# One step of VectorE's exponentials on GpSimd, other buffer counts and another table of the planner's rules

## The chip, the cores and the metric

The kernel runs on one core of a Trainium2 chip. The metric is the device time of one execution in microseconds, as the median of several runs. Names of engines: PE is TensorE, ACT is ScalarE, DVE is VectorE, POOL is GpSimd, SP is SyncE.

## The reference

The input x has 2048 rows of 512 in bf16. The output mixes an attention block and an MLP by a gate for each row:

```python
x = A_x
g = sigmoid((x * gate_w).sum(-1, keepdims=True))
a = attention(x, wqkv, wo)          # 32 heads of 16, softmax over 2048 keys
b = mixer_mlp(x, w1, w2, w3, w4)    # layernorm, gelu(x@w1), shift rows by quarter of channels, @w2,
                                    # residual, layernorm, gelu(@w3) with 1792 columns, @w4, residual
return g * a + (1 - g) * b
```

The attention has 32 x 2048 x 2048 scores, each of which needs an exponential.

## The kernel before

**Units and slots.** The queries are cut into four chunks of 512 and the heads into eight groups of four, which makes 32 units. A unit has 64 blocks of scores: 16 tiles of 128 keys for each of four heads. TensorE computes the scores of two or three blocks into a PSUM tile (`stage`, line 709; function `score`), ScalarE makes the exponentials of that tile in one instruction (`pt`, line 947; 1024 or 1536 elements per partition), and TensorE multiplies them with the values into an accumulator (`acc`, line 960; `attend_block`). One such round is a slot. Two sets of PSUM banks alternate, so the scores of slot k wait for the exponentials of slot k - 2.

**Quad chains.** Some tiles of keys do not go to ScalarE. Their four heads' scores go one by one into a fourth PSUM tile (`dsc`) in slots that then hold only two blocks for ScalarE. VectorE makes their exponentials by working on the bits of bf16 numbers. Function `whole` posts a chain: four dumps (line 873, `dsc` to int16, 512 wide; the bank is free after it), then on all four heads together, 2048 wide, mantissa (883), square (888), power (893) and a last addition of a constant (898, function `later`). Three of these results, the square, the power and the last sum, are each multiplied with the values into the same accumulator. The buffers of a chain (`quad`, and later also parts of `more` and `xT`) come from a list `room`.

**The other work.** TensorE also makes the projections, the MLP's matmuls (line 223) and the output's; VectorE evacuates PSUM, computes the layernorms' statistics (311, 314) and normalized rows (331) as side jobs (`asides`), and rescales each unit's accumulator (1031 to 1051). ScalarE also makes the GELUs (925, 928) in five groups, with table loads around each. GpSimd only sets constants at the start, raises eight small tiles to a power (321) and makes one addition at the end (1156).

**The order.** A planner in the kernel's own Python runs when the program is built. It keeps a clock for each engine (`free`), a cost for each piece of work and a list of what may come next, picks the earliest by time and rank, and emits the instruction. So the order on each engine's queue is fixed by the planner's costs and rules. `USUAL` and `RULES` hold the rules, by unit: how much work of VectorE's may stand in its queue before a new chain starts (`DLIM`), how many chains may run at once (`CHAINS`), from when on tiles of the next unit may be taken (`NEED`), and when a chain's steps and TensorE's products move up (`AHEAD`, `HURRY`, `MANY`, `PTS`). `CREDIT` and `LATER` set how much of the MLP TensorE may do in each slot. Where TensorE would be idle it gets filling matmuls (`fill`, lines 1259 and 1262). `port` keeps two kinds of work apart in time: work posted as shared on VectorE (the 2048-wide steps, the normalized rows, the rescaling) and all work on GpSimd.

Of the kernel before, what the change touches and what calls it, by code (L numbers as in the profile page):

```python
# [12 lines left out]
ALU = mybir.AluOpType  # L13
# [5 lines left out]
I16 = mybir.dt.int16  # L19
# [8 lines left out]
QUARTER = 32.0 - 3.0 * 128.0  # L28
# [4 lines left out]
def kernel(  # L33
# [14 lines left out]
    P = 128  # L48
# [3 lines left out]
    H = 32  # L52
    DH = D // H
    KT = D // P
    VK = 5
    OB = 8
    PTB = 6
    APART = 8
    STAY = 0

    QS = 128.0 * DH ** -0.5 / LN2
    NT = S // P
# [94 lines left out]

    USUAL = {"NEED": 34, "AHEAD": 16, "HURRY": 14, "DLIM": 1.8, "MANY": 5, "PTS": 4, "CHAINS": 3}  # L160
    RULES = {1: {"NEED": 26, "HURRY": 0, "MANY": 5, "PTS": 6, "CHAINS": 3}, 2: {"NEED": 26, "HURRY": 0, "DLIM": 1.5, "MANY": 4, "PTS": 5}, 4: {"AHEAD": 16, "HURRY": 8}, 6: {"AHEAD": 6, "HURRY": 0, "DLIM": 2.1, "MANY": 4, "CHAINS": 4}, 7: {"MANY": 3, "PTS": 6}, 8: {"NEED": 26, "HURRY": 18, "CHAINS": 3}, 9: {"NEED": 36, "HURRY": 8, "DLIM": 2.1, "MANY": 3, "CHAINS": 5}, 10: {"DLIM": 1.2, "MANY": 5, "CHAINS": 4}, 12: {"NEED": 26, "HURRY": 18, "MANY": 2}, 13: {"HURRY": 8, "PTS": 5}, 14: {"NEED": 28, "AHEAD": 16, "HURRY": 24, "CHAINS": 5}, 15: {"AHEAD": 10, "MANY": 2, "PTS": 5}, 16: {"NEED": 28, "AHEAD": 16, "DLIM": 1.8, "MANY": 2}, 18: {"NEED": 30, "AHEAD": 6, "HURRY": 0, "MANY": 5}, 19: {"NEED": 32, "DLIM": 1.5}, 20: {"AHEAD": 8, "DLIM": 2.1, "MANY": 4, "PTS": 3, "CHAINS": 4}, 21: {"NEED": 32, "AHEAD": 16, "HURRY": 8, "PTS": 5}, 22: {"AHEAD": 8, "HURRY": 18, "MANY": 3, "PTS": 5}, 23: {"NEED": 30, "AHEAD": 12, "HURRY": 14, "DLIM": 2.1, "CHAINS": 4}, 24: {"NEED": 34, "AHEAD": 8, "MANY": 4, "PTS": 5}, 27: {"AHEAD": 10, "DLIM": 1.8, "CHAINS": 4}, 28: {"NEED": 26, "DLIM": 1.5, "MANY": 4}, 29: {"AHEAD": 10, "DLIM": 1.5, "MANY": 5, "CHAINS": 3}, 30: {"NEED": 28, "AHEAD": 10, "DLIM": 1.5, "MANY": 4}, 31: {"NEED": 32, "HURRY": 18, "MANY": 5, "PTS": 6, "CHAINS": 5}}
    MM = 0.2235
    TURN = 0.09
    PE_OUT = 0.43
    WARM = 8
    EARLY = 34
    DUNIT = 1
    MAXD = 16
    LASTNEED = 32
    SPLIT = 12  # L170
    RANGES = ((0, 2), (2, 3), (3, 4))
    SPACE = 1
    CREDIT = 0.45
    LATER = 0.4
    GELU, WTWO = 1.0, 1.6
    MOST = 12.0
    LOAD = 1.3
# [3 lines left out]
    SLACK = 0.3  # L181
    AGE = 2.0
    ARANK = 3
    TANH = 1.5
    NOWFREE = 12.0
    free = {"pe": NOWFREE, "act": NOWFREE, "vector": NOWFREE, "pool": NOWFREE}
    queue = {"pe": [], "act": [], "vector": [], "pool": []}
    state = {"n": 0, "gen": 0, "young": True, "mm": 0, "kind": "", "t": 0.0, "piece": 0.0,
             "credit": 0.0, "mixable": 0, "done": False, "ending": False, "acc": 0.0, "accsb": 0.0, "slot": 0, "outs": 0, "bank": 0}
    asides = deque()  # L190
    at = {}
# [365 lines left out]
    def job_option():  # L557

        if current["job"]:
            return 0.0, current["job"]  # L560
        bank = bank_time()
        if bank is None:
            return None
        options = []
        if urgent and urgent[0].hold() is not None:
            options.append((max(urgent[0].hold(), bank), 0, urgent[0]))
        if outs and out_ready(*outs[0])() is not None:
            full = len(oTs) - NU * state["outs"] > NU + 2
# [160 lines left out]
    def scores(start):  # L729
        k = len(slots)  # L730
        if gelus:
            return gelu_slot(start)
        if k == EARLY:
            young.close()
            state["young"] = False
            pools["g"] = ctx.enter_context(tc.tile_pool(name="g", bufs=2))
            late = ctx.enter_context(tc.tile_pool(name="late", bufs=1)).tile([P, CH], BF16, name="late")
            oroom.append(late[:])
        if ends:
            return end_slot(start)  # L740
# [12 lines left out]
        begin = start + (TURN if state["kind"] != "score" else 0.0)  # L753
        rows = [0, 0, 0, 0]
        for i, (n, m) in enumerate(blocks):
            score(st[:, i * CH:(i + 1) * CH], n, m)
            slot_of[(n, m)] = (k, i)
            rows[m % 4] += 1
            first = place["n"] != n
            place["n"], place["m"] = n, m + 1  # L760
            if first:
                unit_begins(n)
            if m // 4 != group.get("kt") or group.get("n") != n:
                close_group()
                group.update(n=n, kt=m // 4, members=[])
            group["members"].append(m)
        following = upcoming(1)
        if not following or following[0][0] != group["n"] or following[0][1] // 4 != group["kt"]:
            close_group()
        slots.append(blocks)  # L770
        state["slot"] = len(slots)
        users[k] = len(blocks)
        if place["n"] == len(units) - 1 and remaining(place["n"]) == SPLIT + 4:
            split()
        if mine:
            n, kt, j = mine
            taken[n].update((kt, i) for i in range(4))
            rows[j] += 1
            score(dsc[:], n, 4 * kt + j)
        spent = max(rows) * MM  # L780
        free["pe"] = begin + spent
        state["kind"] = "score"
        scored[k] = begin + spent - MM + PE_OUT
        if mine:
            dumped[k] = None
            whole(k, dsc, n, kt, j, begin + spent - MM + PE_OUT)
        state["mm"] = 0
        if not state["young"]:
            state["credit"] = min(state["credit"] + (LATER if ("mix", 3) in at else CREDIT), MOST)
# [60 lines left out]
    def whole(k, dsc, n, kt, j, ready):  # L850
# [41 lines left out]
        def power(end):  # L892
            nc.vector.tensor_scalar(out=tiles["once"], in0=bits, scalar1=0x7F80, scalar2=None, op0=ALU.bitwise_and)  # L893
            produce(n, kt, heads, tiles["once"], end, False)
            post("vector", rank(), 0.69, later, end, True)

        def later(end):
            nc.vector.tensor_scalar(out=bits, in0=bits, scalar1=QUARTER, scalar2=None, op0=ALU.add)  # L898
            quad["chains"] -= 1
            produce(n, kt, heads, bits, end, True)  # L900

# [364 lines left out]
    def option(e):  # L1266
# [8 lines left out]
        if e == "vector" and asides:  # L1275
            key = asides[0][2]
            t = 0.0 if key is None else key() if callable(key) else at.get(key)
            if t is not None:
                if asides[0][3]:
# [85 lines left out]
```

## Time and profile before

| | |
|---|---|
| median of 3 runs | 805.58 us (805.29 to 805.96) |
| profiled execution, first to last instruction | 803.7 us |
| granted TensorE clock, mean | 0.997 |
| TensorE busy | 773.4 us, 96% |
| VectorE busy | 760.8 us, 95% |
| ScalarE busy | 787.6 us, 98% |
| GpSimd busy | 19.6 us, 2% |

The profiled execution has its own time, the span from its first to its last instruction; the measured time has 1.9 us more around it. In a row of the profile the part ahead of the bar tells line, engine, operation, what it writes and reads, and how often; behind it stand the busy time in us, the mean length of one in ns, and the idle time of the engine ahead of these instructions with what ended it. In a piece of the timeline the first number is the start and the second the length, both in us. In a row of waits the three numbers are the total in us, how often, and the longest.

### The profile page before, as it was taken

The page shows a single profiled execution, that of the slowest core. Times are in us where ns is not written, and L with a number is a line of the kernel's source. Part 1 is how long each engine was busy: PE and PEld are TensorE (multiplying, and loading weights), DVE is VectorE, ACT ScalarE, POOL GpSimd, SP SyncE. Part 2 cuts the span into 40 slices and gives each one's busy share as a digit, 9 for nine tenths or more (in the row PEclk, how much of TensorE's full clock was granted, in tenths as well). Part 3 has the DMA queues.
Part 4 walks back from the last instruction along what each step waited for, and adds up shares of the span by engine and source line. Part 5 has one row for each costly group of instructions (what it writes and reads, how often), then busy time and mean ns, then how long its engine had stood idle before and what let it go on. Part 6 is the DMA issues. An engine that isn't in the chain of part 4 may idle for free.

```text
span 803.7 us, 15774 instructions
## 1 busy us (share of the span) xinstructions
PE 773.4 (96%) x6332; PEld 245.8 (31%) x6332; DVE 760.8 (95%) x1237; ACT 787.6 (98%) x734; POOL 19.6 (2%) x46
## 2 busy tenths in 40 slices
PE   9999999999999999999999999999999999999997
PEld 3333333332322323232222233222233233322223
DVE  5799999999889999999999997999999999999995
ACT  6999999999999999999999999999999999999996
POOL 4100000000000000010000000000000000000000
PEclk9999999999999999999999999999999999999998
DMA  8700031230100033001000001001001000000000
GB/s 201 179 15 15 16 67 28 41 42 15 42 1 15 15 106 42 15 1 41 15 14 26 18 15 41 15 3 42 13 14 41 15 6 12 21 21 29 15 15 27
DMA packets 48176, 26.41 MB, mean 33 GB/s; under 512 B 34664, under 2 KB 43624, under 8 KB 48104
## 3 DMA queue, kind: packets, MB, share of 16 engines
q1 hardware_dynamic: 47144, 24.90, 13.0%
q8 instruction: 49, 0.80, 0.4%
q10 hardware_dynamic: 960, 0.52, 0.2%
q14 instruction: 23, 0.19, 0.1%
HBM read 17.04 MB, written 2.35 MB: 24 GB/s over the span
## 4 chain that ended last, share of the span: by engine, by line
ACT 59%; issue 21%; PE 17%; DVE 2%; DVEq 0%; ACTq 0%
ACT pt L947 54%; PE stage L709 5%; PE acc L960 4%; PE ps L223 3%; ACT g2T L925 2%; ACT g2T L928 1%; DVE st L311 1%; ACT L925 1%; PE ps_y L223 1%; PE acc L1259 1%; ACT hT L925 1%; PE ps_v L281 1%; PE ps_k L223 1%; PE warm L1177 0%; PE spare L1262 0%
## 5 line engine op out<-in xcount | busy, mean ns | idle before, releaser
L947 ACT ACTIVATE pt<-stage 128x1024 bf16<-128x1024 f32 (+1 forms) x695 | 738.1, 1236 | 2.6 <-PE stage L709 1.2
L709 PE MATMUL stage<-qT,kT 32*128 32x512 bf16 (+2 forms) x1644 | 270.9, 379 | 22.1 <-ACT pt L947 10.8
L873 DVE TENSOR_SCALAR quad<-dsc 128x512 int16<-128x512 f32 x320 | 213.2, 684 | 13.7 <-PE dsc L709 11.8
L709 PE MATMUL dsc<-qT,kT 32*128 32x512 bf16 x428 | 164.5, 384 | 0.0
L960 PE MATMUL acc<-pt,vp 128*17 128x512 bf16 (+3 forms) x1644 | 157.1, 380 | 1.1 <-ACT pt L947 0.8
L709 PEld LDWEIGHTS <-kT 32*128 32x128 bf16 x2072 | 83.5, 91 | 237.1 <-issue 203.8
L960 PEld LDWEIGHTS <-vp 128*17 128x17 bf16 (+1 forms) x2928 | 60.3, 88 | 131.4 <-issue 119.4
L960 PE MATMUL acc<-quad,vp 128*17 128x512 bf16 x884 | 82.7, 382 | 0.3
L1259 PE MATMUL acc<-wq,zero 128*128 128x512 bf16 x216 | 75.9, 387 | 0.0
L223 PE MATMUL ps<-w,g2T 128*128 128x512 bf16 x224 | 68.4, 384 | 0.8 <-DVE x_sb L433 0.8
L898 DVE TENSOR_SCALAR quad<-quad 128x2048 int16<-128x2048 int16 x80 | 54.2, 679 | 0.3
L223 PE MATMUL ps_y<-xnT,w 128*128 128x512 bf16 x176 | 54.1, 384 | 0.1
L873 DVE TENSOR_SCALAR xT<-dsc 128x512 int16<-128x512 f32 x60 | 40.0, 684 | 0.7 <-PE dsc L709 0.4
L888 DVE TENSOR_TENSOR quad<-quad,quad 128x2048 bf16<-128x2048 bf16 x30 | 36.4, 1213 | 0.3
L883 DVE TENSOR_SCALAR quad<-quad 128x2048 int16<-128x2048 int16 x50 | 34.2, 683 | 0.1
L893 DVE TENSOR_SCALAR quad<-quad 128x2048 int16<-128x2048 int16 x50 | 34.1, 682 | 0.1
L873 DVE TENSOR_SCALAR more<-dsc 128x512 int16<-128x512 f32 x48 | 32.2, 686 | 0.9 <-PE dsc L709 0.2
L1259 PEld LDWEIGHTS <-zero 128*128 128x128 bf16 x216 | 19.1, 96 | 44.8 <-issue 41.6
L223 PEld LDWEIGHTS <-g2T 128*128 128x128 bf16 x224 | 16.9, 97 | 33.1 <-issue 27.5
L723 PE MATMUL stage<-xnT,w 128*128 128x512 bf16 x112 | 25.0, 379 | 0.1
L960 PE MATMUL acc<-more,vp 128*17 128x512 bf16 x248 | 24.3, 382 | 0.0
L1031 DVE COPY accsb<-acc 128x512 f32<-128x512 f32 x31 | 21.2, 684 | 1.6 <-PE acc L960 1.3
(145 smaller groups left out, 682.0 us busy)
## 6 DMA issues: line engine op xcount, KB each, us to landing
bcs<-rec_d SPq DMA_DIRECT2D x31, 256.0 KB
w<-in_B_w_dram SPq DMA_DIRECT2D x2, 1792.0 KB
out_dram<-ot SPq DMA_DIRECT2D x15, 128.0 KB
x_sb<-in_A_x_dram SPq DMA_DIRECT2D x14, 128.0 KB
w<-in_B_w_dram SPq DMA_DIRECT2D x2, 512.0 KB
wkv<-in_A_wqkv_dram SPq DMA_DIRECT2D x1, 512.0 KB
wo_pad<-in_A_wo_dram SPq DMA_DIRECT2D x8, 64.0 KB
xnT<-xn SPq DMA_TRANSPOSE x32
```

The costliest lines, as they stand in the source:

```text
L223: nc.tensor.matmul(*args, **kwargs)
L709: nc.tensor.matmul(out, lhsT=kT[G][32 * j:32 * j + 32, cc, o:o + P], rhs=qTs[(c, G)][32 * j:32 * j + 32, a, lo:hi], start=True, stop=True, ...
L723: nc.tensor.matmul(stages[k][:, i * CH:(i + 1) * CH], lhsT=w[:, kt, m * P:(m + 1) * P], rhs=rhs[:, kt, :], start=(kt == 0), stop=(kt == KT ...
L873: nc.vector.tensor_scalar(out=bits[:, r, :], in0=dsc[:], scalar1=SHIFT, scalar2=LOWEST, op0=ALU.add, op1=ALU.max)
L883: nc.vector.tensor_scalar(out=tiles["once"], in0=bits, scalar1=0x7F, scalar2=0x3F00, op0=ALU.bitwise_and, op1=ALU.bitwise_or)
L888: nc.vector.tensor_tensor(out=tiles["twice"].bitcast(BF16), in0=bits.bitcast(BF16), in1=tiles["once"].bitcast(BF16), op=ALU.mult)
L893: nc.vector.tensor_scalar(out=tiles["once"], in0=bits, scalar1=0x7F80, scalar2=None, op0=ALU.bitwise_and)
L898: nc.vector.tensor_scalar(out=bits, in0=bits, scalar1=QUARTER, scalar2=None, op0=ALU.add)
L925: nc.scalar.activation(out=part, in_=part, func=ACT.Gelu_apprx_tanh)
L947: nc.scalar.activation(out=pt[:, 0:w], in_=stages.pop(k)[:, 0:w], func=ACT.Exp, scale=LN2 / 128.0)
L960: nc.tensor.matmul(accs[n][32 * j:32 * j + M, lo:hi], lhsT=lhsT, rhs=p, start=(kt == 0), stop=(kt == NT - 1), skip_group_check=True, tile_ ...
L1259: nc.tensor.matmul(acc[:], lhsT=zero[:], rhs=wq[:, 0, :], start=False, stop=False, skip_group_check=True)
```

## The change

The last step of a quad chain moves from VectorE to GpSimd, as a multiplication by 1.0 and an addition; the planner counts 2.0 us for it. Chains may take the last seven key tiles of a unit instead of the last five (`VK`), and up to 20 blocks of a unit instead of 16 (`MAXD`). The exponentials' tiles have seven buffers instead of six (`PTB`), a chain's list starts with six rooms instead of four, and the MLP's first layer and its hidden activations share one buffer instead of two (`g`). With `STAY` at 1 the products rank higher directly after other products. Side jobs of VectorE gain rank by the time for which they have waited (`LAG`). The MLP may also go on without credit when no room for an output tile is left. The table of rules is another one.

```diff
-    VK = 5
+    VK = 7
     OB = 8
-    PTB = 6
+    PTB = 7
     APART = 8
-    STAY = 0
+    STAY = 1
...
-    USUAL = {"NEED": 34, "AHEAD": 16, "HURRY": 14, "DLIM": 1.8, "MANY": 5, "PTS": 4, "CHAINS": 3}
-    RULES = {1: {"NEED": 26, "HURRY": 0, "MANY": 5, "PTS": 6, "CHAINS": 3}, 2: {...}, ...}
+    USUAL = {"NEED": 34, "AHEAD": 8, "HURRY": 20, "DLIM": 1.2, "MANY": 4, "PTS": 5, "CHAINS": 3}
+    RULES = {1: {"AHEAD": 6, "PTS": 6}, 3: {"AHEAD": 4, "DLIM": 2.5}, 6: {"NEED": 40}, ...}
+    LATE = 2.0
...
-    MAXD = 16
+    MAXD = 20
...
-    CREDIT = 0.45
-    LATER = 0.4
+    CREDIT = 0.5
+    LATER = 0.5
...
+    LAG = 4.0
...
-        if main.hold and main.hold() is not None and (state["young"] or state["credit"] > 0 or not upcoming(1)):
+        if main.hold and main.hold() is not None and (state["young"] or state["credit"] > 0 or not oroom or not upcoming(1)):
...
-    room = deque(epool.tile([P, 4, CH], I16, name=f"quad{i}")[:] for i in range(4))
+    room = deque(epool.tile([P, 4, CH], I16, name=f"quad{i}")[:] for i in range(6))
...
-            pools["g"] = ctx.enter_context(tc.tile_pool(name="g", bufs=2))
+            pools["g"] = ctx.enter_context(tc.tile_pool(name="g", bufs=1))
...
         def power(end):
             nc.vector.tensor_scalar(out=tiles["once"], in0=bits, scalar1=0x7F80, scalar2=None, op0=ALU.bitwise_and)
             produce(n, kt, heads, tiles["once"], end, False)
-            post("vector", rank(), 0.69, later, end, True)
+            post("pool", rank(), LATE, later, end, True)
         def later(end):
-            nc.vector.tensor_scalar(out=bits, in0=bits, scalar1=QUARTER, scalar2=None, op0=ALU.add)
+            nc.gpsimd.tensor_scalar(out=bits, in0=bits, scalar1=1.0, scalar2=QUARTER, op0=ALU.mult, op1=ALU.add)
...
                 if asides[0][3]:
                     t = max(t, port["pool"] - 0.14)
-                options.append((max(f, t), ARANK, 0, None))
+                since = max(t0, state["aside"])
+                options.append((max(f, t), ARANK - max(0.0, max(f, t) - since) / LAG, 0, None))
...
             cost, fn, _, shared = asides.popleft()
+            state["aside"] = start + cost
```

More of the change, by code (lines that the diff above doesn't have):

```diff
@@ L156 @@
     nc.sync.dma_start(out=w3[:], in_=wview(B_w3))
-    USUAL = {"NEED": 34, "AHEAD": 16, "HURRY": 14, "DLIM": 1.8, "MANY": 5, "PTS": 4, "CHAINS": 3}
-    RULES = {1: {"NEED": 26, "HURRY": 0, "MANY": 5, "PTS": 6, "CHAINS": 3}, 2: {"NEED": 26, "HURRY": 0, "DLIM": 1.5, "MANY": 4, "PTS": 5}, 4: {"AHEAD": 16, "HURRY": 8}, 6: {"AHEAD": 6, "HURRY": 0, "DLIM": 2.1, "MANY": 4, "CHAINS": 4}, 7: {"MANY": 3, "PTS": 6}, 8: {"NEED": 26, "HURRY": 18, "CHAINS": 3}, 9: {"NEED": 36, "HURRY": 8, "DLIM": 2.1, "MANY": 3, "CHAINS": 5}, 10: {"DLIM": 1.2, "MANY": 5, "CHAINS": 4}, 12: {"NEED": 26, "HURRY": 18, "MANY": 2}, 13: {"HURRY": 8, "PTS": 5}, 14: {"NEED": 28, "AHEAD": 16, "HURRY": 24, "CHAINS": 5}, 15: {"AHEAD": 10, "MANY": 2, "PTS": 5}, 16: {"NEED": 28, "AHEAD": 16, "DLIM": 1.8, "MANY": 2}, 18: {"NEED": 30, "AHEAD": 6, "HURRY": 0, "MANY": 5}, 19: {"NEED": 32, "DLIM": 1.5}, 20: {"AHEAD": 8, "DLIM": 2.1, "MANY": 4, "PTS": 3, "CHAINS": 4}, 21: {"NEED": 32, "AHEAD": 16, "HURRY": 8, "PTS": 5}, 22: {"AHEAD": 8, "HURRY": 18, "MANY": 3, "PTS": 5}, 23: {"NEED": 30, "AHEAD": 12, "HURRY": 14, "DLIM": 2.1, "CHAINS": 4}, 24: {"NEED": 34, "AHEAD": 8, "MANY": 4, "PTS": 5}, 27: {"AHEAD": 10, "DLIM": 1.8, "CHAINS": 4}, 28: {"NEED": 26, "DLIM": 1.5, "MANY": 4}, 29: {"AHEAD": 10, "DLIM": 1.5, "MANY": 5, "CHAINS": 3}, 30: {"NEED": 28, "AHEAD": 10, "DLIM": 1.5, "MANY": 4}, 31: {"NEED": 32, "HURRY": 18, "MANY": 5, "PTS": 6, "CHAINS": 5}}
+    USUAL = {"NEED": 34, "AHEAD": 8, "HURRY": 20, "DLIM": 1.2, "MANY": 4, "PTS": 5, "CHAINS": 3}
+    RULES = {1: {"AHEAD": 6, "PTS": 6}, 3: {"AHEAD": 4, "DLIM": 2.5}, 6: {"NEED": 40}, 8: {"NEED": 28}, 9: {"PTS": 3, "CHAINS": 5}, 10: {"PTS": 4}, 12: {"AHEAD": 8}, 13: {"AHEAD": 32, "CHAINS": 5, "NEED": 32}, 15: {"MANY": 4}, 18: {"PTS": 4, "DLIM": 1.5}, 19: {"PTS": 6, "HURRY": 18}, 20: {"AHEAD": 20, "DLIM": 2.5}, 21: {"MANY": 8}, 22: {"CHAINS": 5}, 23: {"PTS": 4}, 24: {"PTS": 4}, 26: {"CHAINS": 6}, 27: {"NEED": 30, "HURRY": 24}, 28: {"MANY": 8}, 29: {"AHEAD": 16, "PTS": 4, "NEED": 40}, 30: {"DLIM": 2.1, "HURRY": 0, "PTS": 4, "NEED": 36, "MANY": 3}, 31: {"PTS": 3}}
     MM = 0.2235
+    LATE = 2.0
     TURN = 0.09
@@ L187 @@
     queue = {"pe": [], "act": [], "vector": [], "pool": []}
-    state = {"n": 0, "gen": 0, "young": True, "mm": 0, "kind": "", "t": 0.0, "piece": 0.0,
+    state = {"n": 0, "gen": 0, "young": True, "mm": 0, "aside": 0.0, "kind": "", "t": 0.0, "piece": 0.0,
              "credit": 0.0, "mixable": 0, "done": False, "ending": False, "acc": 0.0, "accsb": 0.0, "slot": 0, "outs": 0, "bank": 0}
@@ L1278, in option @@
             if t is not None:
+                t0 = t
                 if asides[0][3]:
                     t = max(t, port["pool"] - 0.14)
-                options.append((max(f, t), ARANK, 0, None))
+                since = max(t0, state["aside"])
+                options.append((max(f, t), ARANK - max(0.0, max(f, t) - since) / LAG, 0, None))
         if e == "act":
```

## The prediction, made before the changed kernel had run

> **What bounds the kernel now.** I read the page first, then the groups of instructions on ScalarE with shapes kept apart, then single pieces of the timeline, then the waits. The page has three engines near full:
>
> ```profile
> span 803.7 us, 15774 instructions
> ...
> PE 773.4 (96%) x6332; PEld 245.8 (31%) x6332; DVE 760.8 (95%) x1237; ACT 787.6 (98%) x734; POOL 19.6 (2%) x46
> ```
>
> Busy shares cannot say which of the three sets the end. The groups on ScalarE (count, busy us, mean ns) give its work:
>
> ```profile
> L947 ACT ACTIVATE pt<-stage 128x1024 bf16<-128x1024 f32 x465 | 441.7, 1095 | 1.9 <-PE stage L709 1.2 <-PE dsc L709 0.2 <-ACT pt L947 0.2
> L947 ACT ACTIVATE pt<-stage 128x1536 bf16<-128x1536 f32 x230 | 321.5, 1519 | 0.7
> L925 ACT ACTIVATE g2T<-g2T 128x2048 bf16<-128x2048 bf16 x8 | 14.8, 1902 | 0.0
> L928 ACT ACTIVATE g2T<-stage 128x1536 bf16<-128x1536 f32 x8 | 11.1, 1435 | 0.0
> L925 ACT ACT_TABLE_LOAD x5 | 6.4, 1283 | 0.1
> L947 ACT ACT_TABLE_LOAD x5 | 6.4, 1283 | 0.1
> L925 ACT ACTIVATE hT<-hT 128x1536 bf16<-128x1536 bf16 x4 | 5.6, 1470 | 0.0
> L928 ACT ACTIVATE hT<-stage 128x1024 bf16<-128x1024 f32 x2 | 1.9, 1004 | 0.0
> ```
>
> The mean lengths overlap: one exponential starts before the one ahead of it ends. What each costs is the step between starts. From the timeline (start us, length us): two neighbours of 1024, two neighbours of 1536, the first exponentials, and the first instruction after the last one:
>
> ```profile
> 111.83 1.06 ACT L947 ACTIVATE pt<-stage 128x1024 bf16<-128x1024 f32 x1
> 112.73 1.07 ACT L947 ACTIVATE pt<-stage 128x1024 bf16<-128x1024 f32 x1
> 130.07 1.51 ACT L947 ACTIVATE pt<-stage 128x1536 bf16<-128x1536 f32 x1
> 131.40 1.53 ACT L947 ACTIVATE pt<-stage 128x1536 bf16<-128x1536 f32 x1
> 8.99 7.44 ACT L947 ACTIVATE pt<-stage 128x1024 bf16<-128x1024 f32 x8 [0.93 <-PE stage L709]
> 795.38 0.28 ACT L1095 ACTIVATE accsb<-acc 128x128 f32<-128x128 f32 x1 [0.49 <-PE acc L960]
> ```
>
> An exponential of 1024 costs 0.90 us, one of 1536 costs 1.33. So ScalarE needs 465 x 0.903 + 230 x 1.33 = 725.8 us, plus GELU 14.8 + 11.1 + 5.6 + 1.9 = 33.4 and table loads 12.8: 772.0 us. It has from 8.99 to 795.38, 786.4. ScalarE sets the end, and 14.4 us of its stretch are lost in waits so short that the overlap hides them (the rows show 2.6 us of idle). The 9 us ahead and the 8.3 us behind are outside the change. Who makes ScalarE wait is seen one engine back:
>
> ```profile
> PEld L709 <- DVE quad L873: 16.1, 46, 0.5
> PEld L709 <- DVE quad L883: 3.1, 12, 0.4
> PE stage L709 <- ACT pt L947: 10.8, 38, 0.8
> ```
>
> TensorE stands 16.1 us, in 46 pieces, until a dump (the first VectorE step, which frees a PSUM bank) is done, and 3.1 more behind mantissa steps. The 10.8 us of waiting for ScalarE are as they should be. So the 14.4 us come in part from VectorE being late and in part from TensorE's own work.
>
> **The change part by part.** The sum is made against the execution's span of 803.7; the median of 805.58 lies 1.9 above it, and I add differences to the median.
>
> Counts come from the two programs as built. *Chains.* Before there are 107 quad chains (428 dumps), after there are 108. Exponentials go from 465 + 230 to 469 + 226: four of 1536 become 1024, which saves ScalarE 4 x (1.33 - 0.903) = 1.7 us. That is all that its floor moves: 772.0 becomes 770.3.
>
> *VectorE.* These rows hold the step that leaves and the four that one more chain needs:
>
> ```profile
> L898 DVE TENSOR_SCALAR quad<-quad 128x2048 int16<-128x2048 int16 x80 | 54.2, 679 | 0.3
> L898 DVE TENSOR_SCALAR xT<-xT 128x2048 int16<-128x2048 int16 x15 | 10.2, 678 | 0.0
> L898 DVE TENSOR_SCALAR more<-more 128x2048 int16<-128x2048 int16 x12 | 8.2, 681 | 0.0
> L873 DVE TENSOR_SCALAR quad<-dsc 128x512 int16<-128x512 f32 x320 | 213.2, 684 | 13.7 <-PE dsc L709 11.8
> L888 DVE TENSOR_TENSOR quad<-quad,quad 128x2048 bf16<-128x2048 bf16 x30 | 36.4, 1213 | 0.3
> L883 DVE TENSOR_SCALAR quad<-quad 128x2048 int16<-128x2048 int16 x50 | 34.2, 683 | 0.1
> L893 DVE TENSOR_SCALAR quad<-quad 128x2048 int16<-128x2048 int16 x50 | 34.1, 682 | 0.1
> ```
>
> It loses 54.2 + 10.2 + 8.2 = 72.6 us and gains 4 x 0.684 + 0.683 + 1.213 + 0.682 = 5.3: 760.8 - 67.3 = 693.5 us, 86% of the span. None of that is on ScalarE's path by itself; it counts only as dumps that come sooner.
>
> *GpSimd* gets 108 adds over 128x2048 int16. No row has that form. The nearest:
>
> ```profile
> L134 POOL MEMSET wo_pad<- 128x4096 bf16 x1 | 3.7, 3746 | 0.0
> L1156 POOL TENSOR_TENSOR ot<-ot,parts 128x512 bf16<-128x512 f32 x1 | 1.3, 1262 | 435.5 <-DVE xT L1129 435.5
> L139 POOL TENSOR_SCALAR minus<-ident 128x128 bf16<-128x128 bf16 x1 | 0.5, 535 | 0.0
> ```
>
> By the memset's rate one add takes 3746 / 2 = 1.87 us; by the two-input add's, 4 x 1.262 = 5.05. The 535 ns for 128 elements are mostly a fixed cost, so they don't scale. I take 2.0, near the memset, because the add has one input; the planner's own constants for the other two GpSimd operations (1.1 for the power, 1.3 for the add) lie beside rows of 1.02 (below) and 1.26, and its constant here is 2.0. In all 216 us on an engine that was 2% busy. The Trainium skill, GPSIMD Engine Reference, section "Engine selection", calls one-input operations on GpSimd roughly line-rate; the 1.03 cycles per element at 1.2 GHz of its section "Performance versus the Vector engine" give an estimate of 1.76 us, a little under my value, and no run here shows it yet.
>
> *The new wait.* The matmuls of the third product now wait for GpSimd. Behind them on TensorE's queue, which is in order, stand the next scores, and ScalarE waits for those. The cover: in the listing of the old program two exponentials (median) stand between the last step and the first matmul that reads its product, in the new one three. Three are at least 3 x 0.903 = 2.7 us, so at 2.0 us plus a handover the product is there. With the cover gone, each microsecond that the add is late is one for TensorE, up to 108 times.
>
> *The port.* In the trace GpSimd is held while VectorE runs an operation on two SBUF inputs: its power, 1.02 us at the median, took 1.96 when it started inside a square:
>
> ```profile
> L321 POOL TENSOR_TENSOR rstd<-rstd,mhalf x8: 1006/1024/1964, 19.6 to 361.5; 128x4 f32<-128x4 f32 x8
> 286.24 1.23 DVE L888 TENSOR_TENSOR more<-quad,quad 128x2048 bf16<-128x2048 bf16 x1
> 286.37 1.96 POOL L321 TENSOR_TENSOR rstd<-rstd,mhalf 128x4 f32<-128x4 f32 x1 [253.25 <-DVE rstd L320]
> 31.83 1.25 POOL L321 TENSOR_TENSOR rstd<-rstd,mhalf 128x4 f32<-128x4 f32 x1 [3.30 <-DVE rstd L320]
> 32.32 0.73 DVE L331 TENSOR_SCALAR xn<-x_sb,mv,rstd 128x512 bf16<-128x512 bf16 x2
> ```
>
> The reverse is not shown: the normalizing steps at 32.32 ran through the power unhindered (0.73 us for two), but that power touches four elements. The Trainium skill, SBUF — State Buffer, section "SBUF: two separate sides", states the harder rule: the pair is locked for the whole instruction, and the later of the two blocks fully, whichever it is. It would speak against this change. As a mechanism here: if VectorE's 2048-wide steps wait until an add ends, the price follows from the listing. Behind the 108 adds stand 0, 1, 2 or 3 unaffected VectorE instructions (some 0.65 us each) ahead of the next 2048-wide, normalizing or scaling one in 2, 11, 33 and 27 cases, more in the rest. At 2.0 us the waits are 2 x 2.0 + 11 x 1.35 + 33 x 0.7 + 27 x 0.05 = 43 us, and VectorE's 693.5 becomes 737, still under the 760.8 of before. So both with the lock and without it VectorE has more room, if the add takes 2.0.
>
> *TensorE.* Changes between kinds of matmul (scores, products, full ones) go from 1758 to 1691, since products now follow products when they can (STAY). From the timeline, a change costs a step of about 0.33 us, equal ones 0.82 for three, of which the last is 0.39, so 0.215 each:
>
> ```profile
> 652.44 0.82 PE L223 MATMUL ps_y<-xnT,w 128*128 128x512 bf16 x3
> 653.19 0.40 PE L960 MATMUL acc<-pt,vp 128*32 128x512 bf16 x4
> 653.52 0.39 PE L709 MATMUL stage<-qT,kT 32*128 32x512 bf16 x2
> 653.85 0.39 PE L223 MATMUL ps_y<-xnT,w 128*128 128x512 bf16 x1
> ```
>
> 67 x 0.11 = 7.4 us less; the added chain's two groups of products add 0.4, and 14 more filling matmuls (L1259, L1262: 224 to 238) take 3.0 that were idle anyway.
>
> *At no cost:* one g buffer instead of two, since the matmuls that read the old content stand ahead of the new content's on TensorE; six quad rooms and a seventh exponential buffer only take waits away; the side jobs of VectorE (normalizing, statistics) keep their number, and if their new rank put one ahead of a dump it would cost up to 0.67 us, which VectorE's room now covers. SyncE's queue holds the same 176 issues, with transposes, a weight load and the units' small transfers a few places earlier or later; none is on ScalarE's path, and a late one would cost room in the side work alone.
>
> *The sum.* The floor gives -1.7. Of the 14.4 us lost, between 0 and all can come back. I take a fifth, 3 us: the dump waits of 16.1 should shrink by more than half with VectorE at 86%, but most of the time TensorE was busy right up to the late scores, and its 4 us net of relief are thin over 800. 805.6 - 1.7 - 3 = 801 us, between 790 (nothing lost) and 804 (nothing regained).
>
> **The rivals.** *The add holds VectorE.* Place: the 2048-wide steps behind an add. It decides by the add's length. At 2.35 us the waits by the same count reach 2 x 2.35 + 11 x 1.7 + 33 x 1.05 + 27 x 0.4 + 11 x 0 = 69 us, and VectorE is back at 760. At 2.5 it has 2 x 2.5 + 11 x 1.85 + 33 x 1.2 + 27 x 0.55 = 80, 773 us of 803.7; it had 43 us of unavoidable idle (803.7 - 760.8), so the span would be some 816, the median 818. At 3 it would be 836 and more, and the third products would be late too. For it: the two-input row of 5.05 and the lock by the page; against it: the memset row, and no row in which GpSimd holds VectorE. With a milder lock the price is 808 to 818; I take 814. *Nothing comes of it.* The waits are TensorE's, reshuffled by another order: the losses stay at 14 +- 2, the time 804, from 802 to 806. For it: TensorE at 96% and no more than 16.1 us behind dumps.
>
> **The numbers.** The forecast has 0.57, the held VectorE 0.25, nothing 0.18. What a measurement of this kernel can tell from no change is 0.2%, 1.6 us: faster is under 804.0, slower over 807.2. The forecast is faster nearly throughout (0.55, and 0.02 within); of the second rival 0.07 is faster, 0.08 within, 0.03 slower; the first is slower. So 0.62 faster, 0.10 within, 0.28 slower. The range reaches from 794 (half of the losses regained) to 814.
>
> **What would show it.** Right: 469 and 226 exponentials with starts 0.90 and 1.33 apart; L900 on POOL at 1.9 to 2.1 us; VectorE at 690 to 740 us; the dump wait of TensorE under 8 us; ScalarE's last exponential 3 to 6 us earlier. Wrong: L900 at 2.4 us or more, 2048-wide steps of VectorE that take over 0.68 or 1.22 us, or TensorE waiting for POOL ahead of L962.

## The result, and the profile after

The changed kernel takes 808.1 us (median of 8 runs, 807.7 to 810.1), the kernel before 805.5 beside it (8 runs, 805.3 to 807.0): the ratio is 1.003, interval 1.002 to 1.004. It is slower by 0.3%; 801 was forecast. The line numbers of the changed kernel are two higher than those quoted so far (the scores are L711, the exponentials L949, the dumps L875), except for the last step, now L900 on POOL.

The page of the changed kernel, its span and busy times:

```profile
span 806.2 us, 15941 instructions
...
PE 772.4 (96%) x6354; PEld 245.3 (30%) x6354; DVE 723.6 (90%) x1137; ACT 785.9 (97%) x734; POOL 251.5 (31%) x154
```

VectorE has 37 us less to do, and the span is 2.5 us longer. The exponentials by shape, the adds of GpSimd (shortest, median and longest in ns, then where they lie), and three rows of the waits:

```profile
L949 ACT ACTIVATE pt<-stage 128x1024 bf16<-128x1024 f32 x469 | 445.9, 1105 | 5.4 <-PE dsc L711 4.0 <-PE stage L711 1.1
L949 ACT ACTIVATE pt<-stage 128x1536 bf16<-128x1536 f32 x226 | 316.3, 1541 | 1.6 <-PE stage L711 1.1
```

```profile
L900 POOL TENSOR_SCALAR quad<-quad x78: 1897/1901/2880, 50.9 to 788.1; 128x2048 int16<-128x2048 int16 x78
```

```profile
PEld L711 <- DVE quad L875: 13.9, 41, 1.3
...
DVE rec L1045 <- DMA den<-accsb: 4.5, 3, 3.9
...
ACT pt L949 <- PE dsc L711: 4.0, 4, 1.6
```

Counts and add are as forecast: 469 + 226 exponentials, 1.90 us for an add. The waits are not: TensorE still stands 13.9 us behind dumps (16.1 before). One wait is new, VectorE's reciprocal (L1045) for a DMA, 3.9 us at the longest, and one has grown: ScalarE stands 4.0 us in four pieces behind the scores for `dsc` (0.2 us before).

The first exponentials on ScalarE, the last ones, and the first instruction behind them, after:

```profile
9.17 7.44 ACT L949 ACTIVATE pt<-stage 128x1024 bf16<-128x1024 f32 x8 [0.93 <-PE stage L711]
...
792.84 5.54 ACT L949 ACTIVATE pt<-stage 128x1536 bf16<-128x1536 f32 x4
798.86 0.28 ACT L1097 ACTIVATE accsb<-acc 128x128 f32<-128x128 f32 x1 [0.49 <-PE acc L962]
```

The stretch began at 9.17, so it is 789.7 us long, where 786.4 were. ScalarE's need by the prediction's own sum (469 x 0.903 + 226 x 1.33 + 33.4 + 12.8) is 770.3. **19.4 us are lost where 14.4 were.** (With 0.9033 for the step these are 19.3 and 14.2, and the losses below are counted so.) The difference of the two spans is then complete: -1.7 for the floor, +5.0 lost, +0.2 for the later start, -1.0 behind the stretch, together +2.5.

ScalarE's gaps longer than half a microsecond that are new lie at 238, 338, 614 and 616 us. Counted as starts that come too late, they are 0.99, 1.61, 1.72 and 1.03: 5.35 us, a little more than the 5.0. So the 0.3% has four places, and the timeline tells what stood there.

**Around 610 us: an order on SyncE's queue.** The timeline of SyncE, VectorE and ScalarE, in which the bracket is the idle time ahead and what ended it:

```profile
604.08 5.17 SPq L346 DMA_TRANSPOSE xnT<-xn  x4
609.36 0.57 SPq L1038 DMA_DIRECT2D den<-accsb  x1
...
611.24 0.25 DVE L1045 RECIPROCAL rec<-den 128x16 f32<-128x16 f32 x1 [3.87 <-DMA den<-accsb]
611.41 1.82 DVE L875 TENSOR_SCALAR quad<-dsc 128x512 int16<-128x512 f32 x3
...
609.53 2.85 ACT L949 ACTIVATE pt<-stage 128x1024 bf16<-128x1024 f32 x3
613.98 1.02 ACT L949 ACTIVATE pt<-stage 128x1024 bf16<-128x1024 f32 x1 [1.59 <-PE dsc L711]
615.91 1.96 ACT L949 ACTIVATE pt<-stage 128x1024 bf16<-128x1024 f32 x2 [0.91 <-PE dsc L711]
```

Four transposes of the layernorm's rows now stand ahead of the transfer of a unit's denominators, and occupy the queue for 5.17 us. (In the kernel before the transfer went at 602.3 us and the transposes followed at 605.0.) VectorE, which is in order, stands idle for 3.87 us ahead of its reciprocal; the dumps behind it come at 611.41; TensorE has no free `dsc` bank, and ScalarE no scores. The second gap, at 616, has one more cause, which the windows show (columns: window, its length, busy time and instructions of PE, PEld, DVE, ACT and POOL, then the granted TensorE clock and the share and rate of the DMA):

```profile
610.00:612.00 2.00, 0.39 (x2) 0.10 (x3) 0.76 (x3) 2.00 (x3) 0.00 (x0) 1.00 0.04 4
612.00:614.00 2.00, 1.91 (x10) 0.34 (x13) 1.27 (x4) 0.41 (x2) 0.00 (x0) 0.63 0.10 16
614.00:616.00 2.00, 2.00 (x16) 0.38 (x9) 1.45 (x3) 1.09 (x2) 0.00 (x0) 0.52 0.19 72
616.00:618.00 2.00, 2.00 (x15) 0.50 (x13) 1.75 (x3) 2.00 (x3) 0.00 (x0) 1.00 0.16 59
```

TensorE was busy 0.39 us of two, and from 612.5 to 615.9 it had half its clock: it works nearly all of that time and is late with the next scores. That the late scores come from the clock and not from the work is argued from these rows.

**At 332 and 235 us: GpSimd's add holds VectorE.**

```profile
332.46 2.20 POOL L900 TENSOR_SCALAR quad<-quad 128x2048 int16<-128x2048 int16 x1 [11.46 <-DVE quad L895]
332.82 1.87 DVE L322 TENSOR_SCALAR rstd<-mv 128x4 f32<-128x4 f32 x1
...
338.11 1.94 ACT L949 ACTIVATE pt<-stage 128x1024 bf16<-128x1024 f32 x2 [1.35 <-PE dsc L711]
...
232.40 4.18 POOL L900 TENSOR_SCALAR quad<-quad 128x2048 int16<-128x2048 int16 x2 [9.39 <-DVE quad L895]
235.08 2.05 DVE L885 TENSOR_SCALAR quad<-more 128x2048 int16<-128x2048 int16 x1
```

The addition of epsilon to four numbers per partition (L322, usually 0.17 us) starts inside an add and ends with it, at 334.69 against 334.66. It is a side job that the planner's `port` does not know as shared. At 235.08 a mantissa step (0.68 alone) takes 2.05. A held VectorE shows as a longer instruction, not as idle time. The Trainium skill, SBUF — State Buffer, section "SBUF: two separate sides", says of a GpSimd operation and a VectorE operation in a two-port mode (or with two SBUF inputs) that the one which starts first has the shared port pair for its whole instruction and that the other is blocked fully. These rows fit it, down to an operation on four elements.

### The profile page after: what moved, and what is told of

Same layout as the page of the kernel before. It is cut to its first block, busy times and chain, and to the rows that moved or that the text cites. A ratio compares the mean times of both kernels' runs of the same rounds, so it can differ in the third digit from the quotient of the medians.

```text
span 806.2 us, 15941 instructions
## 1 busy us (share of the span) xinstructions
PE 772.4 (96%) x6354; PEld 245.3 (30%) x6354; DVE 723.6 (90%) x1137; ACT 785.9 (97%) x734; POOL 251.5 (31%) x154
## 3 DMA queue, kind: packets, MB, share of 16 engines
HBM read 17.04 MB, written 2.35 MB: 24 GB/s over the span
## 4 chain that ended last, share of the span: by engine, by line
ACT 54%; PE 21%; issue 19%; DVE 5%; SPq 0%; DMA 0%; DVEq 0%; ACTq 0%
ACT pt L949 51%; PE stage L711 6%; PE acc L962 5%; PE ps L225 3%; PE ps_v L283 1%; ACT g2T L927 1%; PE acc L1261 1%; PE stage L725 1%; DVE quad L875 1%; PE ps_o L225 1%; ACT g2T L930 1%; DVE quad L885 1%; PE ps_k L225 1%; SPq L346 0%; ACT L927 0%
## 5 line engine op out<-in xcount | busy, mean ns | idle before, releaser
L949 ACT ACTIVATE pt<-stage 128x1024 bf16<-128x1024 f32 (+1 forms) x695 | 736.4, 1247 | 6.9 <-PE dsc L711 4.0
L900 POOL TENSOR_SCALAR quad<-quad 128x2048 int16<-128x2048 int16 x78 | 168.2, 2156 | 409.4 <-DVE quad L895 375.8
L711 PE MATMUL stage<-qT,kT 32*128 32x512 bf16 (+2 forms) x1640 | 271.3, 380 | 21.9 <-ACT pt L949 11.4
L875 DVE TENSOR_SCALAR quad<-dsc 128x512 int16<-128x512 f32 x312 | 208.4, 685 | 32.1 <-PE dsc L711 30.7
L711 PE MATMUL dsc<-qT,kT 32*128 32x512 bf16 x432 | 166.3, 385 | 1.1 <-DVE quad L875 1.1
L711 PEld LDWEIGHTS <-kT 32*128 32x128 bf16 x2072 | 84.3, 91 | 247.2 <-issue 212.8
L962 PE MATMUL acc<-quad,vp 128*17 128x512 bf16 x1036 | 93.1, 382 | 0.4 <-POOL quad L900 0.3
L1261 PE MATMUL acc<-wq,zero 128*128 128x512 bf16 x232 | 79.5, 386 | 0.0
L890 DVE TENSOR_TENSOR quad<-quad,quad 128x2048 bf16<-128x2048 bf16 x52 | 65.9, 1268 | 0.1
L900 POOL TENSOR_SCALAR more<-more 128x2048 int16<-128x2048 int16 x19 | 40.0, 2104 | 63.4 <-DVE quad L895 59.1
L875 DVE TENSOR_SCALAR more<-dsc 128x512 int16<-128x512 f32 x76 | 50.6, 685 | 5.4 <-PE dsc L711 5.1
L895 DVE TENSOR_SCALAR quad<-quad 128x2048 int16<-128x2048 int16 x72 | 53.6, 748 | 0.1
L885 DVE TENSOR_SCALAR quad<-quad 128x2048 int16<-128x2048 int16 x72 | 49.3, 686 | 0.1
L875 DVE TENSOR_SCALAR xT<-dsc 128x512 int16<-128x512 f32 x44 | 29.7, 686 | 11.5 <-PE dsc L711 11.1
L900 POOL TENSOR_SCALAR xT<-xT 128x2048 int16<-128x2048 int16 x11 | 24.0, 2179 | 49.4 <-DVE quad L895 42.5
L225 PEld LDWEIGHTS <-g2T 128*128 128x128 bf16 x224 | 16.3, 97 | 33.4 <-issue 27.0
```

The costliest lines, as they stand in the source:

```text
L225: nc.tensor.matmul(*args, **kwargs)
L711: nc.tensor.matmul(out, lhsT=kT[G][32 * j:32 * j + 32, cc, o:o + P], rhs=qTs[(c, G)][32 * j:32 * j + 32, a, lo:hi], start=True, stop=True, ...
L875: nc.vector.tensor_scalar(out=bits[:, r, :], in0=dsc[:], scalar1=SHIFT, scalar2=LOWEST, op0=ALU.add, op1=ALU.max)
L890: nc.vector.tensor_tensor(out=tiles["twice"].bitcast(BF16), in0=bits.bitcast(BF16), in1=tiles["once"].bitcast(BF16), op=ALU.mult)
L900: nc.gpsimd.tensor_scalar(out=bits, in0=bits, scalar1=1.0, scalar2=QUARTER, op0=ALU.mult, op1=ALU.add)
L949: nc.scalar.activation(out=pt[:, 0:w], in_=stages.pop(k)[:, 0:w], func=ACT.Exp, scale=LN2 / 128.0)
```

## The experiments

All are of the changed kernel unless said otherwise, and ratios are against the kernel before on the same chip.

### The two causes, each taken away alone, and both

`sp_first` sends the four transposes of one normalization (the second layernorm's last group) only after the next unit's denominators:

```diff
+        def send():
+            for j in range(4):
+                nc.sync.dma_start(out=xnT[...], in_=xns.pop((n, 4 * c + j))[:], transpose=True)
+        if (n, c) == (1, 3):
+            held.append(send)
+        else:
+            send()
 ...  # in the unit's end, behind the transfer of den
+            while held:
+                held.pop()()
```

> The changed kernel with one place of SyncE's queue turned round: the last chunk's four transposes are issued behind the den transfer of the unit that ends there, not ahead of it; every other queue keeps its order. If the den transfer that comes late is one cause (the reciprocal waits 3.9 us, dumps stand behind it, ScalarE loses 1.72 + 1.03 us at 614 and 616 us), the time falls by 2.7 to 805.4 us and the two gaps go. If ScalarE's loss there is TensorE's own order, the time stays at 808.1.

`small_add` lets GpSimd's instruction work on four columns instead of 2048, with the same waits and the same order. The rest of the product lacks its constant:

```diff
-            nc.gpsimd.tensor_scalar(out=bits, in0=bits, scalar1=1.0, ...)
+            nc.gpsimd.tensor_scalar(out=bits[:, 0, 0:4], in0=bits[:, 0, 0:4], scalar1=1.0, ...)
```

> The changed kernel with GpSimd's add cut to 4 of its 2048 columns (the rest of the product lacks its constant); all queues in the same order. If GpSimd's add holds VectorE (17 us of stretched VectorE instructions, two of which cost ScalarE 1.61 us at 338 and 0.99 at 238), no VectorE instruction is stretched, VectorE's busy time falls from 724 to about 700 us and the time by 2.6 to 4 us, to 804.1 to 805.5. If the holds are all covered, the time stays within 0.5 us of 808.1.

`both` has the two edits.

> Both edits, the turned place of SyncE's queue and the add of 4 columns. If the two causes are separate they add up: 808.1 - 2.7 - 2.6 (to 4) = 801.4 to 802.8 us, with ScalarE losing 14 to 15 us as before the change. If one hid behind the other the time stays above 804.

| | time, us (runs) | ratio to before (805.44) | lost by ScalarE |
|---|---|---|---|
| sp_first | 805.6 (11) | 0.9999 (0.999 to 1.0007) | 16.4 |
| small_add | 805.65 (12) | 0.9993 (0.998 to 1.0004) | 17.0 |
| both | 802.85 (6) | 0.9966 (0.995 to 0.998) | 14.1 |

By the medians each is worth about 2.5 us, and together they give 5.2. One reservation: the twelve times of `small_add` lie in two groups, six from 803.8 to 805.0 us with a mean granted clock of 0.999 to 1.000, and six from 806.3 to 806.9 with 0.998. Its trace is of the second group, and there the clock is at half for over 3 us from 611 on, behind the late transfer that `small_add` keeps. `both`, without that transfer, has 802.85. So it seems that the late transfer itself costs some 1.3 us and the clock that falls behind it the rest; no trace of the first group exists to show it.

The timeline of `sp_first` has the transfer first, a reciprocal at 607.74, and eight exponentials without a gap:

```profile
605.79 0.54 SPq L1044 DMA_DIRECT2D den<-accsb  x1
606.42 5.18 SPq L348 DMA_TRANSPOSE xnT<-xn  x4
...
607.74 0.25 DVE L1053 RECIPROCAL rec<-den 128x16 f32<-128x16 f32 x1
...
609.85 7.44 ACT L955 ACTIVATE pt<-stage 128x1024 bf16<-128x1024 f32 x8
```

With both removed the losses are 14.1, those of the kernel before, although VectorE is at 88% (105 matmuls are missing from this trace, so PE's busy time is too small here):

```profile
span 800.9 us, 15853 instructions
...
PE 749.5 (94%) x6249; PEld 244.7 (31%) x6354; DVE 708.0 (88%) x1137; ACT 785.5 (98%) x734; POOL 63.8 (8%) x154
```

So of the 14 us that the kernel before lost, none came back on balance. Whether VectorE's room made good something that the new order costs is not shown. VectorE's busy time is 708.0 where about 700 had been expected.

### Does the place of a held instruction decide, or its length?

Two versions of `sp_first` let VectorE make 3 of the 108 adds. `three_back` takes the two that held the instructions at 235 and 332 us and the one that follows the latter, `three_other` three others that held VectorE by 1.51, 1.33 and 1.70 us at places where ScalarE had not been late:

```diff
+            made.append(0)
+            if len(made) - 1 in (27, 39, 40):      # three_other: (9, 79, 90)
+                nc.vector.tensor_scalar(out=bits, in0=bits, scalar1=QUARTER, scalar2=None, op0=ALU.add)
+            else:
                 nc.gpsimd.tensor_scalar(out=bits, in0=bits, scalar1=1.0, scalar2=QUARTER, ...)
```

> The kernel with the turned place of SyncE's queue (805.6 us), and 3 of the 108 adds made by VectorE again: those ahead of the two places where a held VectorE costs ScalarE 1.62 us at 338 and 0.99 at 238, and the add that follows the first of them. If these places are what the holds cost, VectorE works 2 us longer and both gaps go: 805.6 - 2.6 = 803.0 us, below the kernel before (805.5). If the holds cost in many small pieces, under 0.5 us is gained: 805 or more.

> The same with 3 other adds back on VectorE, ahead of holds that are as long (1.51 us at 119, 1.33 and 1.70 at 605 and 686) but stand ahead of no gap of ScalarE. If a hold costs only where dumps behind it are due, nothing is gained: 805.6 +- 0.5 us. If the length of the holds counts, 803 to 804.

`three_back`: 804.0 us (11 runs) beside 805.35, ratio 0.998 (0.997 to 0.999). `three_other`: 805.5, ratio 0.9999 (0.999 to 1.0008), the same as `sp_first` alone. The place decides. In `three_back` the two VectorE instructions are short, and the gap of 1.35 in front of ScalarE at 338 is 0.25. The time is 1.0 us above the 803.0 expected; ScalarE loses 15.1 us, 1.3 less than in `sp_first`:

```profile
333.06 0.16 DVE L324 TENSOR_SCALAR rstd<-mv 128x4 f32<-128x4 f32 x1
...
235.42 0.68 DVE L892 TENSOR_SCALAR quad<-more 128x2048 int16<-128x2048 int16 x1
...
336.65 1.94 ACT L960 ACTIVATE pt<-stage 128x1024 bf16<-128x1024 f32 x2 [0.25 <-PE dsc L718]
```

`both` apart, which leaves out most of the constant, it is the fastest version here: below both kernels, 0.2% under the one before.

### Mending the held addition in other ways, which failed

`reduce` makes the epsilon addition a reduction over a pair (variance, stored epsilon); `mended` adds the order of `sp_first`:

```diff
 ...  # mvs gets a third column, set to EPS at the start
-            nc.vector.tensor_scalar(out=rstds[n][:, tt], in0=mvs[n][:, tt, 1], scalar1=EPS, scalar2=None, op0=ALU.add)
+            nc.vector.tensor_reduce(out=rstds[n][:, tt], in_=mvs[n][:, tt, 1:3], op=ALU.add, axis=AX.X)
```

> The changed kernel with the four-element addition of the layernorm's epsilon (128x4, held 1.70 us by GpSimd's add at 333 us) made as a reduction over variance and a stored epsilon; all queues in the same order. If that form is not held by GpSimd's add, the gap of 1.61 us on ScalarE at 338 us goes and the time is 806.5 us. If VectorE is held whatever the form, or the loss only moves to the next instruction, 808.1.

> The changed kernel with the turned place of SyncE's queue and the reduction. Both causes separate: 808.1 - 2.6 - 1.6 = 803.9 us, with the add of 2048 columns kept; ScalarE still loses the 0.99 us at 238. That would be below the kernel before (805.5) by its smaller floor alone. If the holds that stay grow when the others go: 805 or more.

`reduce`: 808.6 us beside 805.7, 1.003 (1.002 to 1.004). `mended`: 805.6, 0.9997 (0.999 to 1.0005), where 803.9 was expected. The reduction itself is not held; it takes 0.15 us in the middle of an add. But the next add holds the mantissa step three microseconds later:

```profile
333.16 2.20 POOL L902 TENSOR_SCALAR quad<-quad 128x2048 int16<-128x2048 int16 x1 [11.47 <-DVE quad L897]
333.52 0.15 DVE L324 TENSOR_REDUCE rstd<-mv 128x4 f32<-128x8 f32 x1
...
336.52 1.90 POOL L902 TENSOR_SCALAR more<-more 128x2048 int16<-128x2048 int16 x1
336.77 2.19 DVE L887 TENSOR_SCALAR quad<-quad 128x2048 int16<-128x2048 int16 x1
```

The hold moved on to the next instruction that can be held. ScalarE's gap of 1.61 at 338 becomes one of 0.93 at 340, a new one of 0.53 stands at 116, and 19.6 us are lost (19.3 without the edit).

`sp_split2` and `sp_split4` (both with the order of `sp_first`) cut an add into two of 1024 or four of 512 columns, so that VectorE can go in between:

```diff
+            for r in range(0, 4, 2):               # sp_split4: range(4), one row each
+                nc.gpsimd.tensor_scalar(out=bits[:, r:r + 2, :], in0=bits[:, r:r + 2, :], scalar1=1.0, ...)
```

> The kernel with the turned place of SyncE's queue (805.6 us), and GpSimd's add issued as two instructions of 1024 columns; nothing else moves. If VectorE gets in between the halves, a hold lasts at most about 0.95 us, not 1.9: the gaps of 1.62 us at 338 and 0.99 at 238 shrink to under 0.8 and 0.3, and the time falls by 1.2 to 2 us, to 803.6 to 804.4. If GpSimd keeps its turn through both halves, 805.6.

> The same with four instructions of 512 columns. If VectorE gets in between, holds last 0.5 us at most and the time comes near the kernel with a 4-column add, 802.9 to 803.5 us. If each instruction's fixed cost makes the product late for TensorE, or GpSimd keeps its turn, 805.6 or more.

`sp_split2`: 808.9 us beside 806.85, 1.0035 (1.002 to 1.005). `sp_split4`: 845.5, 1.049 (1.047 to 1.050). The groups of the adds, and the waits of TensorE's products for them, of `sp_split2` and then of `sp_split4`:

```profile
L907 POOL TENSOR_SCALAR quad<-quad x156: 1044/1045/2560, 50.6 to 790.3; 128x1024 int16<-128x1024 int16 x156
...
PE acc L969 <- POOL quad L907: 1.7, 4, 0.5
```

```profile
L907 POOL TENSOR_SCALAR quad<-quad x312: 617/618/2132, 50.8 to 828.5; 128x512 int16<-128x512 int16 x156
...
202.84 3.24 POOL L907 TENSOR_SCALAR quad<-quad 128x512 int16<-128x512 int16 x4 [3.60 <-DVE quad L901]
...
PE acc L969 <- POOL quad L907: 16.4, 34, 1.2
...
ACT pt L956 <- PE dsc L717: 24.3, 46, 1.4
```

Halves do shorten the holds (the gap at 238 is gone, that at 338 is 0.88), but a pair takes 2.17 us at the median and up to 3.7, and small waits elsewhere eat more than was gained: 20.1 us are lost, where `sp_first` lost 16.4. Both expected times, 803.6 to 804.4 and 805.6, were missed. Quarters take 2.7 us a chain at the least and 3.0 at the median, with VectorE's steps let in between. Then TensorE waits for GpSimd 16.4 us in that group alone, ScalarE is idle 24.3 us behind `dsc` scores, and the time is 845. This is what the first rival said of an add of 3 us ("the third products would be late too"); its "836 and more" was worked out from a held VectorE, which the quarters do not test. It says how near that edge the change lies.

### The step without the rest, and the rest without the step

`step_alone` is the kernel before with the last step on GpSimd and 2.0 in the planner; `step_small` is the same with the four columns of `small_add`. `rest_alone` is the changed kernel with the step on VectorE:

```diff
 # step_alone, in the kernel before
-            post("vector", rank(), 0.69, later, end, True)
+            post("pool", rank(), 2.0, later, end, True)
 # rest_alone
-            post("pool", rank(), LATE, later, end, True)
+            post("vector", rank(), 0.69, later, end, True)
 ...  # and the addition itself on nc.gpsimd or nc.vector accordingly
```

> The kernel before with only the last step moved to GpSimd (2.0 for the planner), its old rules and buffers. 107 chains and the same 465 and 230 exponentials, so the same floor for ScalarE. If VectorE's room by itself makes dumps earlier and ScalarE's waits shorter: 802 to 804 us. If ScalarE's 14 us of waits are TensorE's and not VectorE's, as the runs so far say: 804.5 to 806.5, plus what single holds cost, 1 to 4 us: 805 to 810.

> The kernel before with the step on GpSimd alone (842.7 us), its add cut to 4 of 2048 columns (the rest of the product lacks its constant), all queues in the same order. If its 37 us are VectorE held by GpSimd, the time falls below 812. If they are the order that the old rules and the planner's 2.0 us make at the ends of units (products of the last chains stand late in TensorE's queue, ScalarE out of buffers), each of the six large gaps shrinks by 1.9 us at most: 831 to 838 us.

> The changed kernel with the last step back on VectorE (cost 0.69 for the planner), all other edits kept. The planner then makes 100 chains: 437 exponentials of 1024 and 258 of 1536, 13.7 us more for ScalarE than the 108 chains. Theory that the GpSimd step pays for itself in chains: about 808.1 + 13.7 less the 3 to 5 us that holds cost, 817 to 819 us. Rival, that the other edits (rules, buffers) are what cost the time and the step brings nothing: no faster than 820 either way, ScalarE losing 20 us or more in waits.

`few_rooms` is the changed kernel with six exponential buffers and four rooms, as before:

> The changed kernel with the old counts of buffers (six for the exponentials, four quad rooms) under the new rules. The planner makes 102 chains, 445 exponentials of 1024 and 250 of 1536: 10.2 us more for ScalarE. If the buffers only carry chains: 808.1 + 10.2 = 818 us. If they also keep ScalarE running at the ends of units: 825 or more.

| | time, us (runs) | ratio | exponentials | floor | lost |
|---|---|---|---|---|---|
| step_alone | 842.7 (5) | 1.045 (1.0435 to 1.0465) | 465 + 230 | 772.1 | 47.5 |
| step_small | 838.3 (4) | 1.040 (1.038 to 1.042) | 465 + 230 | 772.1 | 44.7 |
| rest_alone | 825.0 (4) | 1.023 (1.021 to 1.025) | 437 + 258 | 784.1 | 19.6 |
| few_rooms | 833.3 (4) | 1.034 (1.032 to 1.036) | 445 + 250 | 780.7 | 33.7 |

`step_alone` was expected at 802 to 810: a bad miss. Waits and timeline show a stall at the units' ends:

```profile
ACT pt L947 <- PE acc L960: 18.8, 6, 5.7
```

```profile
410.44 1.90 POOL L898 TENSOR_SCALAR quad<-quad 128x2048 int16<-128x2048 int16 x1 [3.90 <-DVE xT L893]
412.56 0.39 PE L960 MATMUL acc<-quad,vp 128*17 128x512 bf16 x4
413.39 0.68 DVE L1031 COPY accsb<-acc 128x512 f32<-128x512 f32 x1
414.26 0.83 PE L960 MATMUL acc<-pt,vp 128*32 128x512 bf16 x12
414.75 2.37 ACT L947 ACTIVATE pt<-stage 128x1024 bf16<-128x1024 f32 x2 [5.62 <-PE acc L960]
```

The unit's last chain ends with the add; its products keep the accumulator; the copy to `accsb` waits for them, the next unit's products for the copy, and ScalarE, all of whose buffers are full, for those. `step_small`, with almost no add and the same order, loses nearly as much (44.7), so it is the order that the old rules make of the move, and not the add's length or its hold. The rest of the change is what makes the move bearable: in part the buffers (`few_rooms` has such a stall of 5.1 us at 307; its longest, 5.5 us at 292, is another thing, TensorE waiting 4.46 us for transposed rows), and in part the rules, since with the old buffers the new rules lose 33.7 us where the old ones lose 47.5. Which of the rules does it was not taken apart. But `rest_alone` shows that the rest is no gain of its own: with the step back on VectorE the planner makes 100 chains instead of 108, which costs 13.7 us of floor, and the time is above the 817 to 819 expected. Each half alone is worse than the two together.

### More chains

If 708 us of VectorE leave room, more chains should lower the floor. `dlim18` is `mended` with a planner that lets VectorE's queue be longer before it refuses a chain:

```diff
-    USUAL = {..., "DLIM": 1.2, ...}
+    USUAL = {..., "DLIM": 1.8, ...}
```

> The mended kernel with the general limit of VectorE's backlog at 1.8 in place of 1.2: the planner makes 113 chains, 489 exponentials of 1024 and 206 of 1536, 8.5 us less for ScalarE. If VectorE's room is what the move bought and the rules left it unused, the time is 803.9 - 8.5 = 795.4 us, up to 798 with a few more holds. If TensorE or late dumps take it back, 801 or more, with ScalarE losing over 20 us.

850.4 us, 1.055 (1.053 to 1.057), another bad miss: the floor fell by 8.5 us to 761.9, and 66.9 were lost, half of them again at units' ends (the waits):

```profile
ACT pt L957 <- PE acc L970: 33.9, 4, 16.9
```

## Why the prediction was wrong, by its own steps

- **The step that failed first** is the sentence on SyncE: "none is on ScalarE's path, and a late one would cost room in the side work alone". The transfer of the denominators is in that queue, the reciprocal waits for it on an engine whose queue is in order, and the dumps behind it are on ScalarE's path. It cost 2.9 us of the losses (19.3 to 16.4 in `sp_first`), the stretch at half clock included. The prediction counted "a few places earlier or later"; what counts is the time that those places take, 5.17 us for four transposes. A transpose took 1.25 us in the kernel before as well.
- **The port** was counted for "2048-wide, normalizing or scaling" steps. The instruction that cost most has four elements. And the price was spread over all 108 adds (43 us, which VectorE's room would cover), where the groups of VectorE add up to 16.5 us more (791.0 us against 774.5 in `both`): 25 instructions are longer by 0.1 us or more than the same ones of `small_add`, and only two of them are on the path. The two cost 2.3 us (19.3 to 17.0 in `small_add`). Room on average does not cover a hold at a place where the next dump is already awaited; that is the sentence "which VectorE's room now covers", and it failed too. The rival named the right mechanism, and its size was wrong the other way: 808 to 818 with adds of 2.35 to 2.5 us, where adds of 1.90 us cost 2.3 us of time; 808.1 is the lower end of its "808 to 818" only because the queue's cost came on top. A sign that the prediction named as wrong is there, steps over 0.68 us (the last VectorE step of the chains, 682 before):

```profile
L895 DVE TENSOR_SCALAR quad<-quad 128x2048 int16<-128x2048 int16 x72 | 53.6, 748 | 0.1
```

- **The -3.** The fifth of the 14.4 us that was to come back did not: with both new costs gone, 14.1 are lost (`both`). The second rival had this part right ("the losses stay at 14 +- 2, the time 804"; `both` is 802.85). The dump waits of TensorE went from 16.1 to 13.9 and not under 8. This is the largest term of the miss: the sum had 3 us for it, and the runs show none.
- **VectorE's 693.5** was 708.0 without the holds (`both`). 67.3 us net were taken off a busy time in which overlapping neighbours count once. Added up group by group, VectorE has 840.6 us before and 774.5 in `both`, 66.1 less, while its busy time fell by 52.8. On ScalarE the text had seen this overlap, and on VectorE not.
- **The cover of 2.7 us** held at 1.90 (TensorE waited 0.3 us for GpSimd in the whole run). That the product would be late beyond it is shown by the quarters at 3.0 to 3.2 us.
- **Right** were the add (1.90 for 2.0 taken), the counts, and the floor (-1.7). The range held the time; the likeliest case was on the wrong side.

In one line: 805.5 - 1.7 + 2.9 + 2.3 and -0.8 for the two ends of the span is 808.2; 808.1 was measured. The two ends are those of the two traces.

What stays open is the 14 us that all these versions lose. They lie mostly where TensorE is busy right up to late scores; a version with less work on TensorE in those slots was not tried.

## What to carry to other kernels

When work moves to an engine that shares something with the one relieved, look for the single places where the relieved engine is already awaited: two held instructions there cost 2.3 us, and those held elsewhere cost nothing that these runs show. Sending 3 of 108 adds back was worth 1.6 us, while cutting all of them into pieces cost time. When a scheduler's order changes, read each in-order queue by durations and ask of every transfer who waits for it and what stands behind the waiter. And before expecting an idle engine's room to bring time back, show that the losses are waits for that engine.

## What was not expected of the hardware

- A hold goes by the form of the VectorE instruction and not by its size. Of those in the changed kernel that started inside an add, with most of their usual length still ahead of its end, all 13 `TENSOR_SCALAR`s from SBUF to SBUF and all 3 squares ran longer, down to 128x4 (0.17 to 1.87 us); none of the 103 dumps (which read PSUM) and none of the 22 reciprocals did. The reduction of `reduce` was not held either (0.15 us inside an add).
- A GpSimd addition takes 1.90, 1.045 and 0.618 us for 2048, 1024 and 512 columns, and 0.193 for four: about 0.19 us fixed and 0.83 ns per column (an estimate from these four), so cutting it in four adds 0.57 us.
- TensorE's granted clock fell to half for 3.4 us after pauses of 0.62 and 1.10 us close together (the windows at 610 to 616). The Trainium skill, TensorE: Matmul & The Clock Gate, section "Part 1: The HAM clock gate (the "warmup" mystery)", names the half clock and puts it behind an idle window of about 3.4 us; here TensorE had been busy 2.37 of the 4 us ahead, so less idleness was enough. Between 336 and 338 us of the same trace it was busy 0.69 of 2, and the clock stayed; what decides is not shown (two rows of TensorE's timeline, then the window):

```profile
610.60 0.39 PE L711 MATMUL stage<-qT,kT 32*128 32x512 bf16 x2 [0.62 <-ACT pt L949]
612.09 0.37 PE L711 MATMUL dsc<-qT,kT 32*128 32x512 bf16 x1 [1.10 <-DVE quad L875]
```

```profile
608.00:612.00 4.00, 2.37 (x15) 0.79 (x10) 0.76 (x3) 3.75 (x4) 1.43 (x1) 1.00 0.34 66
```

- The clock was low at the kernel's very end in the profile of before and not in that of after, whose tail is 1.0 us shorter; that the clock is the whole of this is only argued (windows of before, then of after):

```profile
795.00:800.00 5.00, 5.00 (x30) 2.84 (x29) 2.85 (x10) 0.96 (x2) 1.26 (x1) 0.66 0.00 0
```

```profile
798.00:803.00 5.00, 4.14 (x34) 2.45 (x33) 3.81 (x12) 1.34 (x3) 1.27 (x1) 1.00 0.00 0
```
